# A fused attention and two-layer kernel: weight splits of layer 1 moved from GpSimd to ScalarE and VectorE, with a separate buffer for early conversions

## The chip, the cores and the metric

The kernel runs on one core of a Trainium2 chip. The metric is the device time of one execution in microseconds (us), median of three runs: 707.14 us, from 705.8 to 709.77. A core has TensorE (PE in the profile; its weight loads have a row of their own, PEld), VectorE (DVE), ScalarE (ACT), GpSimd (POOL) and SyncE (SP, which here issues nearly all DMAs). Each engine takes its instructions in a fixed order and waits on semaphores for the others.

## The reference, cut to what matters

Attention over 2 batches, 12 heads and 448 positions, with a 12 x 12 mixing of the heads before and after the softmax, gives x of 896 tokens by 768. Two feed-forward layers follow, each 768 to 2048 to 768, each with a pointwise function in the middle:

```python
h = x @ w_in                                 # layer 1
g = h * np.clip(h + 3.0, 0.0, 6.0) / 6.0
x = g @ w_out
h = x @ w_in2                                # layer 2
P = a[0] + a[1]*h + a[2]*h**2 + a[3]*h**3
Q = 1.0 + abs(b[0])*abs(h) + abs(b[1])*h**2
out = (P / (Q + 1e-6)) @ w_out2
```

The weights arrive as 64-bit floats, so each one is two 32-bit words in HBM.

## The kernel before, in words

**Split matmuls.** Every product of two fp32 matrices is done as three matmuls (`mm3`, lines 387 to 389): high part times high part, high times low, low times high. So each weight tile is needed as a rounded high part `wh` and a remainder `wl`.

**Units.** Weights come in units (`units`, line 392). Layer 1 has 16 units "in1" (one for each 128-wide slice f of the 2048) and 18 units "out1" (for each 128-wide output slice c of the 768, three pieces kk of 6, 6 and 4 slices f). Layer 2 has 16 "in2" and 16 "out2". A unit is 128 x 768 values (128 x 512 for kk = 2).

**What is done for a unit.** `load_unit` issues one DMA on SP (768 KB) into `wraw`, which has two buffers. `to_f32` turns 64-bit floats into fp32: one ScalarE pass (line 435) and three VectorE passes (437, 439, 443), into `wf`, which has two buffers. `split_pieces` then makes `wh` and `wl`, three buffers each: for layer 1 on GpSimd (459 the copy, 460 the subtraction), for layer 2 on ScalarE (462) and VectorE (463). Since `wh` and `wl` have three buffers, a unit can be split only after TensorE has finished the unit three places earlier.

**Order of the stages.** Attention runs from 0 to some 234 us in an order written by hand; the first four units of layer 1 are split inside it. Then come the "in1" slices f = 2 to 15 (lines 755 to 761; f = 0 and 1 are begun inside the hand-written order): for each f, 18 matmuls of 384 columns and 18 of 512 into two PSUM banks, which `act1` turns into `gh[f]` and `gl[f]` with ScalarE (561, 565) and VectorE (563, 566). Then come the six "out1" slices c (762 to 777), 96 matmuls each, whose results go to `XH` and `XL` (775 to 777). Layer 2 follows from some 467 us to the end. Outside the hand-written part the order of the instructions of each engine is set by a scheduler when the program is built; it is a fixed list on the chip.

**Early conversions.** `pre_slot` (735) uses the time of layer 1 to convert ten "in2" units of layer 2, f = 2 to 11, from 64-bit to fp32 and to write them back to HBM. Three calls make one conversion: load the raw unit into `wpre` (744), run `to_f32` into a `wf` buffer (748, 749), store it with a DMA (752). It is called once for each f and once for each (c, kk). The buffer is the same two-buffer `wf` that layer 1's own units go through.

**The temporaries of `act1`** come from `tmp` (550), four buffers of 128 x 512: two are used for each half of an f.

Of the kernel before, what the change touches and what calls it, by code (L numbers as in the profile page):

```python
# [7 lines left out]
F32 = mybir.dt.float32  # L8
# [40 lines left out]
def fused_kernel(  # L49
# [334 lines left out]
    pools = {}  # L384
# [7 lines left out]
    units = [("in1", f, 0) for f in range(KF)]  # L392
# [36 lines left out]
    def to_f32(t, n, w):  # L429


        tv = t[:, : 2 * n].rearrange("p (a two) -> p a two", two=2)
        hw, lw = tv[:, :, 1], tv[:, :, 0]
        wi = w.bitcast(I32)
        nc.scalar.activation(out=w, in_=hw.bitcast(F32), func=AF.Copy, scale=2.0**-112)  # L435
        yield
        nc.vector.tensor_scalar(out=wi, in0=wi, scalar1=3, scalar2=None, op0=ALU.logical_shift_left)  # L437
        yield
        nc.vector.scalar_tensor_tensor(  # L439
            out=wi, in0=hw, scalar=icst[:, 0:1], in1=wi, op0=ALU.bitwise_and, op1=ALU.bitwise_or  # L440
        )
        yield
        nc.vector.scalar_tensor_tensor(  # L443
            out=wi, in0=lw, scalar=icst[:, 1:2], in1=wi, op0=ALU.logical_shift_right, op1=ALU.bitwise_or
        )
        yield

    def split_pieces(u):
        t, n = raws.pop(u)
        n *= 128  # L450
        if u[0] == "in2" and u[1] in pre:
            w = t
        else:
            w = pools["late"].tile([128, KD * 128], F32, tag="wf", bufs=2, name="wf")[:, :n]
            yield from to_f32(t, n, w)
        hv = pools["late"].tile([128, KD * 128], F32R, tag="wh", bufs=3, name="wh")[:, :n]
        lv = pools["late"].tile([128, KD * 128], F32R, tag="wl", bufs=3, name="wl")[:, :n]
        if u[0] in ("in1", "out1"):
            nc.gpsimd.tensor_scalar(out=hv, in0=w, scalar1=1.0, scalar2=0.0, op0=ALU.mult, op1=ALU.add)  # L459
            nc.gpsimd.tensor_tensor(out=lv, in0=w, in1=hv.bitcast(F32), op=ALU.subtract)  # L460
        else:
            nc.scalar.activation(out=hv, in_=w, func=AF.Copy)
            nc.vector.tensor_tensor(out=lv, in0=w, in1=hv.bitcast(F32), op=ALU.subtract)  # L463
        if u[0] == "out2":
            for d, x in zip(wsp[u[1]], (hv, lv)):
                nc.sync.dma_start(out=d, in_=x.bitcast(F32))
        else:
            hv, lv = (x.rearrange("p (a b) -> p a b", b=128) for x in (hv, lv))
        spl[u] = (hv, lv)

    def split_unit(u):
        for _ in split_pieces(u):
            pass
# [74 lines left out]
            pass  # L548

    def tmp(name, n):  # L550
        return pools["gp"].tile([128, 512], F32, tag="tmp", bufs=4, name=name)[:, :n]

    def act1(f, p):
        t0, t1 = PARTS[p]
        n = t1 - t0
        hp = hps.pop((f, p))[:, :n]
        if f not in gh:
            gh[f] = pools["gp"].tile([128, NT], F32R, tag=f"gh{f}", name=f"gh{f}")
            gl[f] = pools["gp"].tile([128, NT], F32R, tag=f"gl{f}", name=f"gl{f}")
        t = tmp("t1", n)  # L560
        nc.scalar.activation(out=t, in_=hp, func=AF.Relu, bias=bias3)
        g = tmp("g1", n)
        nc.vector.scalar_tensor_tensor(out=g, in0=t, scalar=6.0, in1=hp, op0=ALU.min, op1=ALU.mult)  # L563
        o = gh[f][:, t0:t1]
        nc.scalar.activation(out=o, in_=g, func=AF.Copy)  # L565
        nc.vector.tensor_tensor(out=gl[f][:, t0:t1], in0=g, in1=o.bitcast(F32), op=ALU.subtract)  # L566
# [19 lines left out]
    for C, (b, r0, n, G) in enumerate(chunks):  # L586
# [21 lines left out]
        for s in range(G):  # L608
# [51 lines left out]
            if C == PRE and s == LATE - 1:  # L660
                flush()
                front.release()
                pools["late"] = tc.alloc_tile_pool(name="late", bufs=1, side="right", reuse_waits="tile")
                load_units(1)
                wpieces = (p for u in units[:4] for p in split_pieces(u))
# [46 lines left out]
    gp = pools["gp"] = tc.alloc_tile_pool(name="gp", bufs=1, reuse_waits="tile")  # L712
# [20 lines left out]
    slot, held = [0], {}  # L733

    def pre_slot():
        i, k = divmod(slot[0] - 1, 3)
        slot[0] += 1
        if not 0 <= i < len(PRE2):
            return
        f = PRE2[i]  # L740
        n = KD * 128
        if k == 0:
            held["t"] = gp.tile([128, 2 * n], I32, tag="wpre", name=f"wpre{f}")
            nc.sync.dma_start(
                out=held["t"].rearrange("p (a b) -> p a b", b=256), in_=w2i[:, :, f * 256 : f * 256 + 256]
            )
        elif k == 1:
            held["w"] = pools["late"].tile([128, n], F32, tag="wf", bufs=2, name="wf")
            for _ in to_f32(held["t"], n, held["w"]):
                pass  # L750
        else:
            nc.sync.dma_start(out=pre[f], in_=held["w"])

    ui = 2
    for f in range(2, KF):
        advance(ui)
        for p in range(2):
            run(gemm1(f, p, bank(f"h1_{f}_{p}")))
            act1(f, p)
        pre_slot()  # L760
        ui += 1
    for c in range(KD):
        hp = [bank(f"y1_{c}_{p}") for p in range(2)]
        for kk, (k0, k1) in enumerate(KSP):
            advance(ui)
            wh, wl = spl.pop(("out1", c, kk))
            for f in range(k0, k1):
                for p, (t0, t1) in enumerate(PARTS):
                    mm3(hp[p][:, : t1 - t0], wh[:, f - k0, :], wl[:, f - k0, :], gh[f][:, t0:t1], gl[f][:, t0:t1],
                        f == 0, f == KF - 1)  # L770
            pre_slot()
            ui += 1
        for p, (t0, t1) in enumerate(PARTS):
            y = tmp("y", t1 - t0)
            nc.scalar.activation(out=y, in_=hp[p][:, : t1 - t0], func=AF.Copy, scale=1.0 / 6.0)
            nc.vector.tensor_copy(out=XH[:, c, t0:t1], in_=y)
            nc.vector.tensor_tensor(out=XL[:, c, t0:t1], in0=y, in1=XH[:, c, t0:t1].bitcast(F32), op=ALU.subtract)
# [5 lines left out]
    gp = pools["gp2"] = tc.alloc_tile_pool(name="gp2", bufs=1, reuse_waits="tile")  # L783
# [57 lines left out]
    for f in range(KF):  # L841
        advance(ui, AHEAD2)
        w = spl.pop(("in2", f, 0))
# [155 lines left out]
```

## Time and profile before

| | |
|---|---|
| median of 3 runs | 707.14 us (705.8 to 709.77) |
| the profiled execution | 707.37 us |
| its span in the trace | 705.66 us |
| granted TensorE clock over the span | 0.998 of full speed |
| TensorE busy | 689.6 us, 98% |
| VectorE busy | 557.2 us, 79% |
| ScalarE busy | 411.1 us, 58% |
| GpSimd busy | 256.9 us, 36% (none after some 463 us) |

Three stretches matter. From 244.4 to 346.4 us TensorE does f = 2 to 15 of "in1" (called the h stretch here), from 346.4 to 467.5 us the "out1" slices (the y stretch), and from 467.5 us to the end layer 2. In the rows, tile names of the first stretch are `h`, `g`, `gh`, `gl`; of the second `y`. A time behind "<-" in square brackets is how long the engine was idle before an instruction, and for what it waited. A matmul's row lasts longer than the step to the next one, since matmuls overlap; the step is read from the start times.

### The profile page before, as it was taken

To read this page: it belongs to the slowest core of one execution; us is meant where nothing else is said; L and a number is where in the kernel's file an instruction comes from. 1 tells how busy PE (TensorE), PEld (TensorE's weight loads), DVE (VectorE), ACT (ScalarE), POOL (GpSimd) and SP (SyncE) were. 2 spreads that over 40 slices of the span, in tenths; PEclk is the share of its full clock that TensorE was granted. 3 is DMA by queue.
4 is the path that set the end of the run, shared out by engine and by line. 5 is a ranking of instruction groups with operands and counts; after the bars stand their busy time and mean duration, and the time that the engine had idled before them with its cause. 6 is when DMAs were issued, how large, how long until landed. Compare 5 with 4: busy or idle time off the path is not lost.

```text
span 705.7 us, 12410 instructions
## 1 busy us (share of the span) xinstructions
PE 689.6 (98%) x4461; PEld 617.5 (88%) x4461; DVE 557.2 (79%) x934; ACT 411.1 (58%) x851; POOL 256.9 (36%) x255
## 2 busy tenths in 40 slices
PE   8989999999999999999999999999999999999997
PEld 4768888888889888989888888889999999999997
DVE  6845585665657689889987777879999899989991
ACT  6757887887787343434342212227766667679851
POOL 2876775877776334323434543410000000000000
PEclk9999999999999999999999999999999999999999
DMA  5636486545394444555345544466575584755522
GB/s 206 226 111 176 142 209 190 166 142 166 119 260 123 148 144 136 155 157 156 121 151 177 186 160 141 140 247 236 209 270 186 196 267 144 242 196 202 188 82 89
DMA packets 76032, 122.81 MB, mean 174 GB/s; under 512 B 6804, under 2 KB 56260, under 8 KB 75972
## 3 DMA queue, kind: packets, MB, share of 16 engines
q1 hardware_dynamic: 75684, 121.66, 53.9%
q8 instruction: 35, 0.57, 0.3%
q10 hardware_dynamic: 288, 0.37, 0.1%
q14 instruction: 25, 0.20, 0.1%
HBM read 83.39 MB, written 19.27 MB: 145 GB/s over the span
## 4 chain that ended last, share of the span: by engine, by line
PE 60%; DVE 24%; DMA 7%; ACT 4%; issue 4%; POOL 0%; POOLq 0%; SPq 0%; ACTq 0%; DVEq 0%
PE A L341 9%; DVE wf L439 6%; PE h L389 6%; PE h L388 6%; PE h L387 6%; DVE wf L443 6%; PE acc L387 6%; PE acc L389 6%; PE acc L388 6%; PE X L363 5%; DMA pre<-wf 4%; PE sc L271 4%; DVE gl L566 4%; PE M L306 3%; DVE wf L437 3%
## 5 line engine op out<-in xcount | busy, mean ns | idle before, releaser
L389 PE MATMUL h<-xh,wl 128*128 128x512 f32 (+1 forms) x384 | 139.9, 364 | 0.8 <-DVE wl L463 0.8
L388 PE MATMUL h<-xl,wh 128*128 128x512 f32 (+1 forms) x384 | 139.5, 363 | 0.0
L387 PE MATMUL h<-xh,wh 128*128 128x512 f32 (+1 forms) x384 | 139.5, 363 | 0.0
L435 ACT ACTIVATE wf<-wraw 128x768 f32<-128x768 f32 (+1 forms) x56 | 48.7, 878 | 96.0 <-DMA pre<-wf 57.2
L296 POOL TENSOR_TENSOR sl<-full,sh 120x448 fp32r<-120x448 f32 x87 | 99.9, 1148 | 7.2
L310 DVE TENSOR_REDUCE st<-M 120x1 f32<-120x448 f32 x90 | 56.1, 623 | 51.3 <-PE M L308 51.1
L341 PEld LDWEIGHTS A<-wr,e 120*112 120x112 f32 x720 | 87.2, 178 | 7.9 <-ACT wr L325 3.9
L341 PE MATMUL A<-wr,e 120*112 120x120 f32 x720 | 89.7, 268 | 2.2 <-ACT wr L325 2.2
L459 POOL TENSOR_SCALAR wh<-wf 128x768 fp32r<-128x768 f32 (+1 forms) x34 | 32.6, 959 | 141.4 <-DVE wf L443 140.5
L312 ACT ACTIVATE e<-M,st 120x448 f32<-120x448 f32 x90 | 57.1, 635 | 42.7 <-DVE st L310 37.1
L389 PEld LDWEIGHTS h<-xh,wl 128*128 128x128 f32 x384 | 72.0, 188 | 9.0 <-DVE wl L463 1.1
L387 PEld LDWEIGHTS h<-xh,wh 128*128 128x128 f32 x384 | 72.1, 188 | 7.5
L388 PEld LDWEIGHTS h<-xl,wh 128*128 128x128 f32 x384 | 72.1, 188 | 7.6
L389 PE MATMUL y<-gh,wl 128*128 128x384 f32 x192 | 70.1, 365 | 2.6 <-POOL wl L460 2.6
L388 PE MATMUL y<-gl,wh 128*128 128x384 f32 x192 | 70.2, 366 | 1.0 <-DVE gl L566 1.0
L294 POOL TENSOR_SCALAR sh<-full 120x448 fp32r<-120x448 f32 x87 | 54.3, 624 | 46.1 <-PE M L307 21.5
L387 PE MATMUL y<-gh,wh 128*128 128x384 f32 x192 | 69.9, 364 | 0.0
L460 POOL TENSOR_TENSOR wl<-wf,wh 128x768 fp32r<-128x768 f32 (+1 forms) x34 | 67.5, 1985 | 2.8
L439 DVE SCALAR_TENSOR_TENSOR wf<-wraw,icst,wf 128x768 int32<-128x768 int32 (+1 forms) x56 | 61.7, 1103 | 0.7
L437 DVE TENSOR_SCALAR wf<-wf 128x768 int32<-128x768 int32 x66 | 43.1, 654 | 22.6 <-ACT wf L435 22.3
L443 DVE SCALAR_TENSOR_TENSOR wf<-wraw,icst,wf 128x768 int32<-128x768 int32 (+1 forms) x56 | 57.7, 1032 | 0.6
L565 ACT ACTIVATE gh<-g 128x384 fp32r<-128x384 f32 (+1 forms) x32 | 18.5, 579 | 60.3 <-DVE g L563 60.0
(114 smaller groups left out, 1521.7 us busy)
## 6 DMA issues: line engine op xcount, KB each, us to landing
wraw<-in_moe_w_out_dram SPq DMA_DIRECT2D x28, 768.0 KB
wraw<-in_moe_w_in_dram SPq DMA_DIRECT2D x22, 768.0 KB
full<-stg SPq DMA_DIRECT2D x60, 210.0 KB
vraw<-in_v_dram SPq DMA_DIRECT2D x42, 224.0 KB
wpre<-in_moe_w_in_dram SPq DMA_DIRECT2D x10, 768.0 KB
w2h<-wh SPq DMA_DIRECT2D x16, 384.0 KB
w2l<-wl SPq DMA_DIRECT2D x16, 384.0 KB
ws<-w2h SPq DMA_DIRECT2D x16, 384.0 KB
```

What stands on the lines that cost most here:

```text
L294: eng.tensor_scalar(out=sh[:r], in0=s[:r], scalar1=1.0, scalar2=0.0, op0=ALU.mult, op1=ALU.add)
L296: return lambda: eng.tensor_tensor(out=sl[:r], in0=s[:r], in1=sh[:r].bitcast(F32), op=ALU.subtract)
L310: nc.vector.tensor_reduce(out=st[:r, 0:1], in_=mt[:r, :S], op=ALU.max, axis=AX.X, negate=True)
L312: nc.scalar.activation(out=e[:r], in_=mt[:r, :S], func=AF.Exp, bias=st[:r, 0:1], accum_out=st[:r, 1:2])
L341: nc.tensor.matmul(av[:, jc], lhsT=e[:r, jc * JP : (jc + 1) * JP], rhs=wr[:r, :, :rr], start=True, stop=True)
L387: nc.tensor.matmul(o, lhsT=wh, rhs=mh, start=first, stop=False)
L388: nc.tensor.matmul(o, lhsT=wh, rhs=ml, start=False, stop=False)
L389: nc.tensor.matmul(o, lhsT=wl, rhs=mh, start=False, stop=last)
L437: nc.vector.tensor_scalar(out=wi, in0=wi, scalar1=3, scalar2=None, op0=ALU.logical_shift_left)
L439: nc.vector.scalar_tensor_tensor(out=wi, in0=hw, scalar=icst[:, 0:1], in1=wi, op0=ALU.bitwise_and, op1=ALU.bitwise_or)
L443: nc.vector.scalar_tensor_tensor(out=wi, in0=lw, scalar=icst[:, 1:2], in1=wi, op0=ALU.logical_shift_right, op1=ALU.bitwise_or)
L460: nc.gpsimd.tensor_tensor(out=lv, in0=w, in1=hv.bitcast(F32), op=ALU.subtract)
```

## The change

Three lines change. Only the first four units of layer 1 are still split on GpSimd; the other 12 "in1" units and all 18 "out1" units are split by ScalarE (line 462) and VectorE (463), as those of layer 2 already were. The early conversions write to a buffer `wfp` of their own, one of 128 x 768 in the pool `gp`, instead of a `wf` buffer. To make room in `gp`, `tmp` has three buffers instead of four.

```diff
@@ split_pieces
-        if u[0] in ("in1", "out1"):
+        if u in units[:4]:
             nc.gpsimd.tensor_scalar(out=hv, in0=w, scalar1=1.0, scalar2=0.0, op0=ALU.mult, op1=ALU.add)
             nc.gpsimd.tensor_tensor(out=lv, in0=w, in1=hv.bitcast(F32), op=ALU.subtract)
         else:
             nc.scalar.activation(out=hv, in_=w, func=AF.Copy)
             nc.vector.tensor_tensor(out=lv, in0=w, in1=hv.bitcast(F32), op=ALU.subtract)
@@ tmp
-        return pools["gp"].tile([128, 512], F32, tag="tmp", bufs=4, name=name)[:, :n]
+        return pools["gp"].tile([128, 512], F32, tag="tmp", bufs=3, name=name)[:, :n]
@@ pre_slot
-            held["w"] = pools["late"].tile([128, n], F32, tag="wf", bufs=2, name="wf")
+            held["w"] = gp.tile([128, n], F32, tag="wfp", name="wfp")
```

The order of TensorE's instructions stays as it was. On VectorE, ScalarE and SP it changes inside layer 1. First VectorE in the h stretch, around the second half of f = 9 (`g_4102` and `gl_4074` are its activation; `wpre_4639` is the raw data of an early conversion; a minus is a row of before, a plus one of now):

```order
 L566 TENSOR_TENSOR gl_4074<-g_4077,gh_4073 128x384
-L437 TENSOR_SCALAR wf<-wf 128x768
-L439 SCALAR_TENSOR_TENSOR wf<-wraw,icst,wf 128x768
-L443 SCALAR_TENSOR_TENSOR wf<-wraw,icst,wf 128x768
+L437 TENSOR_SCALAR wfp<-wfp 128x768
+L439 SCALAR_TENSOR_TENSOR wfp<-wpre_4639,icst,wfp 128x768
+L463 TENSOR_TENSOR wl<-wf,wh 128x768
 L563 SCALAR_TENSOR_TENSOR g_4102<-t_4100,h_9_1_4081 128x512
+L443 SCALAR_TENSOR_TENSOR wfp<-wpre_4639,icst,wfp 128x768
 L566 TENSOR_TENSOR gl_4074<-g_4102,gh_4073 128x512
```

An early conversion that stood in the y stretch before (`wpre_4639` is the sixth) now stands here, and a subtraction L463 for each unit is new. In the order of now all ten early conversions stand ahead of the last `gl` of f = 15; in the order of before five do.

Next VectorE in the y stretch, between the results of c = 3 and of c = 4 (`wpre_5227` is the tenth early conversion, 128x512 is a piece kk = 2):

```order
-L437 TENSOR_SCALAR wf<-wf 128x768
-L439 SCALAR_TENSOR_TENSOR wf<-wpre_5227,icst,wf 128x768
-L443 SCALAR_TENSOR_TENSOR wf<-wpre_5227,icst,wf 128x768
+L463 TENSOR_TENSOR wl<-wf,wh 128x768
 L437 TENSOR_SCALAR wf<-wf 128x512
 L439 SCALAR_TENSOR_TENSOR wf<-wraw,icst,wf 128x512
-L437 TENSOR_SCALAR wf<-wf 128x768
 L443 SCALAR_TENSOR_TENSOR wf<-wraw,icst,wf 128x512
+L463 TENSOR_TENSOR wl<-wf,wh 128x768
+L437 TENSOR_SCALAR wf<-wf 128x768
```

The conversion is gone from here and each unit's subtraction stands in the list between the conversions of later units.

Last ScalarE at the same place (L775 writes the results of c = 4 out of PSUM):

```order
-L435 ACTIVATE wf<-wpre_5227 128x768
+L462 ACTIVATE wh<-wf 128x768
 L435 ACTIVATE wf<-wraw 128x512
+L462 ACTIVATE wh<-wf 128x768
 L435 ACTIVATE wf<-wraw 128x768
 L775 ACTIVATE y<-y_4_0_5090 128x384
+L462 ACTIVATE wh<-wf 128x512
 L775 ACTIVATE y<-y_4_1_5091 128x512
```

The ScalarE pass of the early conversion, which stood in front of those of the layer's own units, is gone from here, and the copies to `wh` are new.

On SP the ten pairs of a store and a raw load of the early conversions move with them: they stand one or two loads of layer 1 apart instead of three, and the 12 loads of "out1" after the last store have none between them. Behind the last `gl` of f = 15 no order of layer 2 changes.

## Rows read from the trace of the kernel before

**Rows 1.** Busy time by stretch: TensorE, weight loads, VectorE, ScalarE, GpSimd; clock, DMA share, GB/s.
```profile
244.40:346.40 102.00, 102.00 (x506) 91.28 (x505) 91.45 (x98) 41.06 (x67) 39.58 (x27) 1.00 0.50 151
346.40:467.50 121.10, 117.55 (x578) 103.71 (x577) 99.55 (x105) 29.93 (x45) 51.44 (x34) 1.00 0.51 166
467.50:705.70 238.20, 233.47 (x1250) 220.62 (x1248) 210.97 (x328) 157.63 (x264) 0.00 (x0) 1.00 0.56 194
```
**Rows 2.** Timeline of TensorE: start, length, instruction; the first matmuls of f = 8 and 9.
```profile
302.60 0.33 PE L387 MATMUL h<-xh,wh 128*128 128x384 f32 x1
...
309.87 0.33 PE L387 MATMUL h<-xh,wh 128*128 128x384 f32 x1
```
**Rows 3.** Waits from 222 to 476 us: who for whom, us, times, longest.
```profile
PEld y L389 <- POOL wl L460: 4.2, 5, 1.1
...
PE y L389 <- POOL wl L460: 2.6, 5, 0.8
...
PEld y L388 <- DVE gl L566: 1.4, 1, 1.4
...
PEld h L389 <- DVE wl L463: 1.1, 1, 1.1
...
PE y L388 <- DVE gl L566: 1.0, 1, 1.0
PE h L389 <- DVE wl L463: 0.8, 1, 0.8
```
**Rows 4.** Timeline of TensorE at the start of c = 4 of "out1".
```profile
421.56 0.34 PE L387 MATMUL y<-gh,wh 128*128 128x384 f32 x1
421.73 0.34 PE L388 MATMUL y<-gl,wh 128*128 128x384 f32 x1
422.88 0.44 PE L389 MATMUL y<-gh,wl 128*128 128x384 f32 x1 [0.81 <-POOL wl L460]
```
**Rows 5.** Waits from 345 to 467 us.
```profile
ACT wf L435 <- DMA pre<-wf: 50.3, 6, 10.2
```
**Rows 6.** Chain of waits: start, us, what.
```profile
357.51 5.80 DMA wraw<-in_moe_w_out_dram
```
**Rows 7.** Timeline of VectorE, then of GpSimd at the same time.
```profile
258.99 0.69 DVE L566 TENSOR_TENSOR gl<-g,gh 128x512 fp32r<-128x512 f32 x1 [0.23 <-ACT gh L565]
...
295.59 0.55 DVE L437 TENSOR_SCALAR wf<-wf 128x768 int32<-128x768 int32 x1
...
297.45 0.55 DVE L566 TENSOR_TENSOR gl<-g,gh 128x384 fp32r<-128x384 f32 x1
...
300.26 2.32 DVE L566 TENSOR_TENSOR gl<-g,gh 128x512 fp32r<-128x512 f32 x1
...
300.01 2.02 POOL L460 TENSOR_TENSOR wl<-wf,wh 128x768 fp32r<-128x768 f32 x1
```
**Rows 8.** Groups of VectorE in the h stretch: busy us, mean ns, idle before.
```profile
L566 DVE TENSOR_TENSOR gl<-g,gh 128x512 fp32r<-128x512 f32 x13 | 22.5, 1734 | 4.9 <-ACT gh L565 4.9
L439 DVE SCALAR_TENSOR_TENSOR wf<-wraw,icst,wf 128x768 int32<-128x768 int32 x13 | 19.0, 1460 | 0.2
L437 DVE TENSOR_SCALAR wf<-wf 128x768 int32<-128x768 int32 x17 | 13.0, 762 | 0.0
L443 DVE SCALAR_TENSOR_TENSOR wf<-wraw,icst,wf 128x768 int32<-128x768 int32 x12 | 12.2, 1013 | 0.1
...
L566 DVE TENSOR_TENSOR gl<-g,gh 128x384 fp32r<-128x384 f32 x11 | 7.7, 699 | 0.0
L563 DVE SCALAR_TENSOR_TENSOR g<-t,h 128x384 f32<-128x384 f32 x12 | 6.6, 546 | 5.8 <-ACT t L561 5.8
L439 DVE SCALAR_TENSOR_TENSOR wf<-wpre,icst,wf 128x768 int32<-128x768 int32 x4 | 4.4, 1108 | 0.0
```
**Rows 9.** Groups of VectorE in the y stretch.
```profile
L443 DVE SCALAR_TENSOR_TENSOR wf<-wpre,icst,wf 128x768 int32<-128x768 int32 x6 | 13.5, 2242 | 0.2
...
L439 DVE SCALAR_TENSOR_TENSOR wf<-wpre,icst,wf 128x768 int32<-128x768 int32 x6 | 8.3, 1382 | 0.2
```
**Rows 10.** The splits of layer 2: duration ns, shortest, median, longest.
```profile
L463 DVE TENSOR_TENSOR wl<-wf,wh x22: 948/952/959, 467.9 to 624.7; 128x768 fp32r<-128x768 f32 x22
L462 ACT ACTIVATE wh<-wf x22: 837/848/859, 465.2 to 623.8; 128x768 fp32r<-128x768 f32 x22
```

## The prediction

> **What bounds the kernel now.** I read the busy times by stretch first, then the start times of TensorE's matmuls, then its waits, and only then the engines that it waits for. TensorE is busy for all 102.0 us of the h stretch and for 117.6 of the 121.1 us of the y stretch, at the full granted clock of 1.00 (its 2.4 GHz level) [rows 1]. "Busy" could hide gaps, so the start times are the check: one f begins at 302.60 us and the next at 309.87 [rows 2]. That is 7.27 us, and 14 times that is 101.8 us, so the h stretch of 102.0 us is 14 steps of this length and almost nothing else. TensorE therefore sets the time there, although VectorE is busy for 91.5 of the 102.0 us and GpSimd's work lengthens it.
>
> In the y stretch TensorE does wait. Five waits for GpSimd's `wl` (2.6 us together), one for VectorE's last `gl` (1.0) and one for the `wl` of the first unit of layer 2 (0.8) make 4.4 us [rows 3]. A matmul's row covers part of a gap: at 421.73 us the next matmul begins 1.15 us later where the step is 0.17 (421.56 to 421.73), so 0.98 us is lost and the wait row says 0.81 [rows 4]. With 0.17 us more for each of the seven waits the loss is 4.4 + 1.2 = 5.6 us. The weight loads put their own waits at 4.2 + 1.4 + 1.1 = 6.7 us [rows 3], the other end. What stands behind these waits is not GpSimd's speed alone: ScalarE stood still for 50.3 us in the y stretch, since its conversion pass L435 wanted a `wf` buffer that an early conversion's store still read [rows 5], and whatever came behind in its fixed order stood with it.
>
> **The separate buffer.** Now that store holds only `wfp`, so the 50.3 us of waiting go. In the y stretch no early conversion is left, so VectorE sheds two groups of 13.5 and 8.3 us there [rows 9]. The first subtraction of each c no longer waits for anything that ends shortly before it is needed. With three buffers, a unit is split as soon as TensorE has finished the unit three places earlier, which leaves two units of lead: in the h stretch 2 x 7.27 = 14.5 us; in the y stretch 121.1 less 5.6 us over 96 slices is 1.2 us a slice, and two units are at least 10 slices, 12 us. In the new order the L463 stand at those places, so five waits fall from 3.4 us (2.6 + 5 x 0.17) to nothing. The wait for `gl` of f = 15 (1.2 us) came from VectorE and ScalarE being late at the end of the h stretch behind a weight load of 5.80 us that ScalarE stood at [rows 6]. The first unit of layer 2 (1.0 us) was split late for the same chain of late `wf` buffers. Both should go.
>
> **The splits on VectorE and ScalarE.** This is the step that could cost. GpSimd's subtraction stretches VectorE's instructions when they overlap: the 512-wide `gl` takes 0.69 us alone and 2.32 while GpSimd's L460 runs [rows 7]. In the h stretch this is, from the group means [rows 8] less what the same form takes free [rows 7], for L439 the 1013 ns of L443: 13 x (1734 - 690) = 13.6 us, 13 x (1460 - 1013) = 5.8, 17 x (762 - 550) = 3.6, 11 x (699 - 550) = 1.6, 4 x (1108 - 1013) = 0.4, together 25.0 us. Free of it VectorE needs 91.5 - 25.0 = 66.5 us. Added are 14 subtractions of 0.95 us [rows 10], 13.3 us, and six early conversions that came later before (four had run in this stretch [rows 8]), 6 x (0.55 + 1.01 + 1.01) = 15.4 us. The sum is 95.2 us of 102.0: VectorE stays about as full as before, with the same kind of slack. Its idle time behind ScalarE was 4.9 + 5.8 = 10.7 us [rows 8]; if all of that stays, it needs 105.9 us and ends the stretch 3.9 us late, well inside the lead of 14.5 us. The unit prices that I take are those at the bottom of their rows; their top ends are the third rival below.
>
> ScalarE goes from 41.1 us [rows 1] by 14 x 0.85 [rows 10] and six passes of about 0.9 (estimate: the same 768 values as L462) to some 58 of 102.0 us. Its fixed order is the real risk: a copy to `wh` waits until TensorE has released the buffer, and the activation of the next half stands behind it. In the order that wait ends with the same half of f that the activation wants, so it costs about the copy itself, 0.85 us, with 14.5 us in hand.
>
> In the y stretch VectorE loses at least 21.8 us and gains some 12 x 0.95 + 6 x 0.7 (estimate for 512 columns, 0.95 x 512/768 and a little) = 15.6, out of 99.6 of 121.1 us: no bound.
>
> **The transfers.** Six more early conversions in the h stretch are 6 x (768 + 384) KB = 7.1 MB in 102 us, 69 GB/s on top of 151; layer 2 runs at 194 as a mean [rows 1]. On SP a store waits for its conversion, and the loads behind it wait too. A load issued late by such a wait of 3 or 4 us and then taking 5.80 us is still inside the 14.5 us that two buffers allow. I cost it at nothing; without that cover it would be some 2 to 3 us for each of a few units.
>
> **tmp with three buffers.** A half's first temporary now waits for the `gl` of two halves before; that is done half an f or more earlier. Nothing.
>
> **Sum.** 707.37 us of the profiled execution less 5.6 is 701.8. I keep 0.2 us for small waits that take their place and forecast 702.0 us. Against the median of 707.14, which the profiled execution meets within 0.03%, that is 0.7% less. Its own range from the two ends of the waits (4.4 and 6.7 us) and some 0.7 us of spread is 700.0 to 703.7.
>
> **TensorE's headroom, read in another way.** The rows show the step of 7.27 us with GpSimd and VectorE busy beside it, and weight loads at 91.3 of 102.0 us [rows 1, 2]. The Trainium skill (Perfetto Trace Analysis, Identifying the Most-Contended Engine) holds matmul busy time to be a poor measure of TensorE's headroom and takes the busy share of the weight loads instead. By that rule TensorE has 10.7 us free in the h stretch and 17.4 in the y stretch, and a change that relieves its suppliers could win up to 28 us. By the rows, layer 2, where GpSimd does nothing, has 1250 matmuls in 238.2 us, 0.19 us each beside 0.20 (102.0 / 506) in the h stretch, where more of them have 512 columns; relieved of GpSimd the step is no shorter.
>
> **Rivals.**
> 1. *The wait moves instead of going.* `wl` now comes from an engine with a fixed order, so L463 can be stuck behind conversions whose data are late. The five waits then stay in part, or a few appear in the h stretch. For it: VectorE at 95 of 102 us, and the early conversions as a cycle of store, load and conversion that ScalarE stands at. Against it: leads of 12 us and more. Half the gain lost gives 704.6, all of it 707.
> 2. *Faster by more than the waits.* TensorE speeds up once its suppliers are ahead; up to 28 us as worked out above, 679 us. Against it stands the unvarying step.
> 3. *Slower: VectorE becomes the bound of the h stretch.* If the long forms are not GpSimd's doing (DMA writes or TensorE's reads instead), the 25.0 us stay and VectorE needs 91.5 + 13.3 + 15.4 + 10.7 = 130.9 us of 102.0. It is 28.9 us late; 14.5 are covered, 14.4 are lost, and with the y stretch's gain kept the time is 707.4 + 14.4 - 3.4 = 718 us. It decides from about half of the 25.0 us on (118.4 us needed, 16.4 late, 1.9 lost). Against it: the long `gl` begins with GpSimd's L460 and ends with it [rows 7].
>
> **How the numbers follow.** The forecast has 0.70, rival 1 0.17, rival 2 0.03, rival 3 0.10. What a measurement here can tell from no change is about 0.5%, so "faster" means below 703.6 us: 0.64 of the forecast's 0.70, 0.02 of rival 1 and rival 2's 0.03 give 0.69. "Slower" is above 710.7, rival 3 with little else: 0.09. The rest, 0.22, is the same. For eight in ten I reach from 700.0 to 705.6, which takes in the forecast's own range and the better half of rival 1, and leaves out rivals 2 and 3.
>
> **What would show it.** In the profile after, the waits of TensorE's matmuls for `wl` and `gl` in the y stretch should be gone, an f should still take 7.27 us, and the y stretch should last some 116.5 us instead of 121.1. The 512-wide `gl` should take 0.69 us throughout after the fourth unit, VectorE be busy for some 95 of the 102 us of the h stretch and at most 93 us of the y stretch (99.6 - 21.8 + 15.6), and ScalarE's wait for the store be gone. I am wrong if TensorE waits in the h stretch, if its step changes, or if the y stretch keeps gaps at the start of each c.

## The result, and the profile after

The first measurement gave 698.39 us (median of 4 runs, 697.88 to 701.0) against 706.77 us for the kernel before: a ratio of 0.988, 95% interval 0.984 to 0.992. That is 3.6 us below the forecast and 1.6 us below the low end of its range. A second measurement (e4 below, the same kernel, 6 runs beside 23 of before) gave 700.68 us, ratio 0.991 (0.990 to 0.993), a gain of 6.1 us, inside the range. Both intervals lie below 1. One execution each of e5 (848 us), e8 (1135 us) and e10 (3203 us) was in a slow state and is left out of the times and ratios below. The profiled execution after took 697.88 us with a span of 696.1 us.

The busy times by stretch answer to [rows 1], with the same columns: TensorE, weight loads, VectorE, ScalarE, GpSimd, clock, DMA share, GB/s. The h stretch, the y stretch and layer 2:

```profile
241.63:343.63 102.00, 102.00 (x506) 91.52 (x506) 97.34 (x136) 58.23 (x90) 3.25 (x2) 1.00 0.68 211
343.63:459.49 115.86, 115.86 (x578) 104.01 (x576) 70.31 (x99) 36.46 (x52) 0.00 (x0) 1.00 0.41 138
459.49:696.10 236.61, 233.16 (x1249) 220.65 (x1247) 208.73 (x325) 156.57 (x263) 0.00 (x0) 1.00 0.54 187
```

The h stretch is as long as before, with VectorE even fuller (97.3 of 102 us). The y stretch lasts 115.86 us instead of 121.1, all of it TensorE's own work, and layer 2 is 1.6 us shorter. The waits from 220 to 476 us, which answer to [rows 3] and [rows 5]; these are the two largest of ScalarE, the largest of VectorE, and ScalarE's wait for the loads of the early conversions:

```profile
ACT wh L462 <- PE y L388: 46.6, 10, 6.4
ACT wf L435 <- DVE wl L463: 34.0, 25, 3.3
DVE wl L463 <- ACT wh L462: 30.5, 9, 6.3
...
ACT wfp L435 <- DMA wpre<-in_moe_w_in_dram: 12.5, 8, 3.0
```

No row with TensorE waiting is left, and the wait for a store is gone. ScalarE now stands at its copies until TensorE gives a `wh` buffer back (46.6 us): the suppliers wait for TensorE, and not the other way. The same three matmuls as in [rows 4], now:

```profile
416.05 0.34 PE L387 MATMUL y<-gh,wh 128*128 128x384 f32 x1
416.22 0.34 PE L388 MATMUL y<-gl,wh 128*128 128x384 f32 x1
416.40 0.34 PE L389 MATMUL y<-gh,wl 128*128 128x384 f32 x1
416.57 0.39 PE L387 MATMUL y<-gh,wh 128*128 128x512 f32 x1
```

The fourth row is the next matmul. The step before L389 is 0.18 us, where it was 1.15. ([Rows 4] were labelled wrongly ahead of the prediction: they are not the start of c = 4 but of the last piece, kk = 2, of c = 3. The five waits for `wl` stand at the piece kk = 2 of c = 1 to 5, the one unit of 128x512.) VectorE's groups in the h stretch answer to [rows 8]:

```profile
L463 DVE TENSOR_TENSOR wl<-wf,wh 128x768 fp32r<-128x768 f32 x14 | 15.0, 1068 | 0.0
...
L566 DVE TENSOR_TENSOR gl<-g,gh 128x512 fp32r<-128x512 f32 x14 | 9.6, 688 | 0.0
...
L439 DVE SCALAR_TENSOR_TENSOR wfp<-wpre,icst,wfp 128x768 int32<-128x768 int32 x9 | 9.4, 1045 | 0.2
...
L437 DVE TENSOR_SCALAR wf<-wf 128x768 int32<-128x768 int32 x13 | 7.2, 554 | 1.2 <-ACT wf L435 1.2
L566 DVE TENSOR_TENSOR gl<-g,gh 128x384 fp32r<-128x384 f32 x13 | 7.2, 551 | 0.3 <-ACT gh L565 0.3
```

All the stretched forms are short again: `gl` of 512 columns takes 0.69 us where its mean was 1.73.

**Where the profiled difference of 9.6 us (705.7 to 696.1) comes from.** Read from start times: 2.6 us ahead of the first matmul of `h` (at 222.80 us before, 220.23 after), 0.3 from there to the first `y`, 5.2 in the y stretch, 1.1 at the first unit of layer 2, and 0.4 behind it. The first of these is not the change's. At 36 to 40 us, in the attention part, TensorE waits for GpSimd's L294, and in some executions the granted clock falls behind that. Columns as above, before and then after:

```profile
36.00:40.00 4.00, 1.17 (x7) 0.59 (x6) 1.16 (x4) 1.01 (x3) 1.74 (x3) 1.00 0.76 232
40.00:46.00 6.00, 5.98 (x33) 4.82 (x34) 2.64 (x9) 3.88 (x10) 5.67 (x8) 0.72 0.01 3
```

```profile
36.00:40.00 4.00, 2.47 (x18) 1.86 (x18) 1.93 (x5) 1.09 (x4) 2.66 (x4) 1.00 0.74 232
40.00:46.00 6.00, 5.93 (x43) 4.61 (x43) 3.32 (x12) 4.45 (x13) 5.75 (x8) 1.00 0.06 16
```

In the execution before TensorE was busy for 1.17 of 4 us there, and the clock of the next 6 us was 0.72; after, 2.47 of 4 and 1.00. Inside those 6 us the clock before was near its lower level of 1.2 GHz for a time:

```profile
41.00:44.60 3.60, 3.60 (x18) 2.85 (x17) 1.53 (x8) 2.87 (x8) 3.43 (x5) 0.53 0.02 5
```

The second profiled execution of the changed kernel (e4) has 0.72 again from 40 to 46 us, and starts `h` at 223.09 us. So this is chance from one execution to the next, and the profiled pair overstates the gain by some 2.6 us.

### The profile page after: what moved, and what is told of

It is laid out like the page before. It is cut to its first block, busy times and chain, and to the rows that moved or that the text cites. A ratio compares the mean times of both kernels' runs of the same rounds, so it can differ in the third digit from the quotient of the medians.

```text
span 696.1 us, 12343 instructions
## 1 busy us (share of the span) xinstructions
PE 686.3 (99%) x4460; PEld 616.2 (89%) x4461; DVE 532.7 (77%) x964; ACT 433.8 (62%) x881; POOL 168.2 (24%) x195
## 4 chain that ended last, share of the span: by engine, by line
PE 93%; DMA 2%; DVE 2%; issue 1%; ACT 1%; POOL 0%; SPq 0%; POOLq 0%; DVEq 0%
PE h L389 11%; PE h L388 11%; PE h L387 11%; PE A L341 9%; PE acc L387 6%; PE acc L389 6%; PE acc L388 6%; PE y L388 6%; PE y L387 6%; PE y L389 6%; PE X L363 5%; PE sc L271 4%; PE M L306 3%; PE M L308 2%; PE M L307 2%; DMA vraw<-in_v_dram 1%
## 5 line engine op out<-in xcount | busy, mean ns | idle before, releaser
L389 PE MATMUL h<-xh,wl 128*128 128x512 f32 (+1 forms) x384 | 139.7, 364 | 0.0
L462 ACT ACTIVATE wh<-wf 128x768 fp32r<-128x768 f32 (+1 forms) x52 | 42.6, 819 | 62.0 <-PE y L388 46.6
L389 PEld LDWEIGHTS h<-xh,wl 128*128 128x128 f32 x384 | 72.1, 188 | 7.6
L435 ACT ACTIVATE wf<-wraw 128x768 f32<-128x768 f32 (+1 forms) x56 | 49.5, 883 | 42.9 <-DVE wl L463 40.8
L463 DVE TENSOR_TENSOR wl<-wf,wh 128x768 fp32r<-128x768 f32 (+1 forms) x52 | 49.6, 954 | 32.4 <-ACT wh L462 32.4
L389 PE MATMUL y<-gh,wl 128*128 128x384 f32 x192 | 69.5, 362 | 0.0
L294 POOL TENSOR_SCALAR sh<-full 120x448 fp32r<-120x448 f32 x87 | 54.0, 620 | 43.5 <-PE M L307 20.6
L443 DVE SCALAR_TENSOR_TENSOR wf<-wraw,icst,wf 128x768 int32<-128x768 int32 (+1 forms) x56 | 56.5, 1011 | 0.7
L439 DVE SCALAR_TENSOR_TENSOR wf<-wraw,icst,wf 128x768 int32<-128x768 int32 (+1 forms) x56 | 55.9, 999 | 0.9
L348 ACT ACTIVATE at<-A 112x480 f32<-112x480 f32 x87 | 50.3, 579 | 1.8 <-PE A L341 1.8
L389 PE MATMUL acc<-ws,xl 128*128 128x384 f32 x128 | 42.8, 334 | 0.0
```

The lines of the kernel that those rows point to most:

```text
L294: eng.tensor_scalar(out=sh[:r], in0=s[:r], scalar1=1.0, scalar2=0.0, op0=ALU.mult, op1=ALU.add)
L348: aposts.append(lambda: nc.scalar.activation(out=o, in_=av, func=AF.Copy))
L389: nc.tensor.matmul(o, lhsT=wl, rhs=mh, start=False, stop=last)
L439: nc.vector.scalar_tensor_tensor(out=wi, in0=hw, scalar=icst[:, 0:1], in1=wi, op0=ALU.bitwise_and, op1=ALU.bitwise_or)
L443: nc.vector.scalar_tensor_tensor(out=wi, in0=lw, scalar=icst[:, 1:2], in1=wi, op0=ALU.logical_shift_right, op1=ALU.bitwise_or)
```

## The experiments

All on whole kernels, five rounds each unless said; ratios to the kernel before, which ran beside them (706.78 us with e1 to e4, 706.67 with e5 to e8, 706.37 with e9 to e11).

| run | us | ratio, 95% interval |
|---|---|---|
| e1 split edit alone | 699.84 | 0.991, 0.9895 to 0.9925 |
| e2 separate buffer (and `tmp` of three) alone | 707.5 | 1.0015, 0.9995 to 1.0036 |
| e3 `tmp` of three alone | 707.04 | 1.0008, 0.999 to 1.0025 |
| e4 the whole change again | 700.68 | 0.9914, 0.9897 to 0.9932 |
| e5 split edit, GpSimd subtracts for nothing | 717.4 | 1.0152, 1.0131 to 1.0173 |
| e6 whole, GpSimd copies `wh` | 699.48 | 0.9897, 0.9878 to 0.9917 |
| e7 whole, V loaded later | 699.49 | 0.9895, 0.9877 to 0.9913 |
| e8 whole, filler matmuls | 699.12 | 0.9898, 0.9878 to 0.9919 |
| e9 as e5, one round | 716.62 | 1.0141, 1.0106 to 1.0177 |
| e10 whole, GpSimd subtracts `wl` | 708.38 | 1.0029, 1.0013 to 1.0044 |
| e11 whole, each subtraction three times | 707.34 | 1.0011, 0.9992 to 1.0031 |

### Which edit does it: e1 to e4

Theory A is the prediction's: the waits come from the `wf` buffer that an early conversion's store still reads. Theory B: they come from GpSimd. e1 has only this line of the change, e3 only `tmp`, e2 `tmp` and the buffer:

```diff
e1  -        if u[0] in ("in1", "out1"):
    +        if u in units[:4]:
e3  -  tag="tmp", bufs=4
    +  tag="tmp", bufs=3
e2  as e3, and
    -            held["w"] = pools["late"].tile([128, n], F32, tag="wf", bufs=2, name="wf")
    +            held["w"] = gp.tile([128, n], F32, tag="wfp", name="wfp")
```

> Only the splits move to ScalarE and VectorE; the early conversions keep sharing the wf buffers and stay half in the y stretch. Theory A (the waits of TensorE in the y stretch come from the wf buffer that a store still reads): ScalarE still stands some 50 us for the store, most of the waits for wl stay, and the time is 704 to 707 us. Theory B (they come from GpSimd, which is slow and stretches VectorE): the waits are gone although ScalarE still stands for the store, and the time is that of the whole change, 698 to 699 us.

> Only the separate buffer and the three temporaries; all splits of layer 1 stay on GpSimd. Theory A: the waits of the y stretch fall by most of their 4.6 us of gaps; in the h stretch VectorE needs some 91.5 + 15.4 + 10.7 = 117.6 us of 102.0 with GpSimd's stretching still there, 1 us over the lead of 14.5 us, so 701 to 704 us. Theory B: the waits for GpSimd's wl stay and the time is 706 to 708 us.

> Only three temporaries instead of four. The lists of all engines stay as in the kernel before, so both theories expect no change, 706 to 707.5 us; it also shows how far two programs with the same lists differ, and how often TensorE's clock falls in the attention part (by half for 3.4 us in the profile of before, not in that of after), which I hold for chance: some of its executions should have it and some not.

> The whole change once more, timed closely. By the gaps of TensorE that went (6.5 us with the longer matmul behind each) the ratio should be 0.989 to 0.992 of before; a ratio of 0.988 or less would say that about 2 us more come from elsewhere, such as the attention part, where the profile of after is 2.6 us shorter.

The split edit alone gives the whole gain, and the separate buffer alone gives nothing. In e1 no wait of TensorE is left from 220 to 476 us, and its y stretch lasts 115.85 us. Although the early conversions still go through `wf`, the 50.3 us of [rows 5] are down to this (waits from 345 to 467 us of e1, then ScalarE at the conversion of the piece kk = 2 of c = 1):

```profile
ACT wf L435 <- DMA pre<-wf: 1.1, 4, 0.3
```

```profile
359.35 1.70 ACT L435 ACTIVATE wf<-wraw 128x512 f32<-128x512 f32 x2 [0.24 <-DMA pre<-wf]
```

This conversion begins 15.6 us after the first matmul of the y stretch (343.80 us); in the kernel before it began 29.3 us after it (375.76 and 346.48). Ahead of it ScalarE now has a copy at which it waits for TensorE (44.0 us for all copies from 345 to 467 us), and by then the store has landed. So the long wait for the store went together with the lateness of the whole chain, and no other buffer was needed to take it away; Theory A, that the buffer is what matters, falls. (Theory B had the time nearly right, but not that the store wait would go.) With e2 the five waits at kk = 2 do go, which Theory B had not foreseen either, but others take their place. TensorE's waits of e2 from 300 to 476 us, and the stretch in which they lie:

```profile
PE y L388 <- DVE gl L566: 1.8, 2, 1.6
PE y L387 <- DVE g L563: 1.0, 1, 1.0
PE y L387 <- ACT gh L565: 0.6, 1, 0.6
PE y L389 <- POOL wl L460: 0.4, 1, 0.4
```

```profile
344.00:372.00 28.00, 24.12 (x108) 20.11 (x107) 27.43 (x34) 11.74 (x19) 9.29 (x9) 0.95 0.41 135
```

TensorE is busy for 24.12 of these 28 us and VectorE for 27.43: VectorE is late with the last `g` and `gl`, which TensorE wants at the start of the y stretch. The buffer lets the early conversions run in the h stretch, and there GpSimd's subtraction stretches them. VectorE's groups of e2 in the h stretch (beside those of after, above):

```profile
L566 DVE TENSOR_TENSOR gl<-g,gh 128x512 fp32r<-128x512 f32 x12 | 13.8, 1146 | 0.0
L439 DVE SCALAR_TENSOR_TENSOR wf<-wraw,icst,wf 128x768 int32<-128x768 int32 x12 | 13.7, 1143 | 0.2
L439 DVE SCALAR_TENSOR_TENSOR wfp<-wpre,icst,wfp 128x768 int32<-128x768 int32 x8 | 13.2, 1653 | 0.2
```

`wfp` takes 1.65 us where it takes 1.05 in the changed kernel. The longest of the new waits ends with such a stretched instruction; TensorE, VectorE and GpSimd in e2:

```profile
368.61 0.50 PE L388 MATMUL y<-gl,wh 128*128 128x512 f32 x1 [1.60 <-DVE gl L566]
```

```profile
366.49 2.06 DVE L566 TENSOR_TENSOR gl<-g,gh 128x512 fp32r<-128x512 f32 x1 [0.16 <-ACT gh L565]
...
365.98 2.03 POOL L460 TENSOR_TENSOR wl<-wf,wh 128x768 fp32r<-128x768 f32 x1
```

At its 0.69 us this `gl` would have been there 1.4 us earlier. How the five waits of before came about can be followed in its trace; here for c = 1, kk = 2, one row each of ScalarE, VectorE and GpSimd, and of TensorE the late matmul and its next:

```profile
375.76 1.46 ACT L435 ACTIVATE wf<-wraw 128x512 f32<-128x512 f32 x2 [9.39 <-DMA pre<-wf]
...
378.05 0.74 DVE L443 SCALAR_TENSOR_TENSOR wf<-wraw,icst,wf 128x512 int32<-128x512 int32 x1
...
378.96 1.25 POOL L459 TENSOR_SCALAR wh<-wf 128x512 fp32r<-128x512 f32 x1 [6.86 <-DVE wf L443]
380.29 1.87 POOL L460 TENSOR_TENSOR wl<-wf,wh 128x512 fp32r<-128x512 f32 x1
...
382.21 0.44 PE L389 MATMUL y<-gh,wl 128*128 128x384 f32 x1 [0.15 <-POOL wl L460]
382.50 0.40 PE L387 MATMUL y<-gh,wh 128*128 128x512 f32 x1
```

The store, the conversion and then 1.25 + 1.87 us on GpSimd stand in one chain that ends at TensorE. Either edit removes these five waits; only the split edit brings no new ones. Whether the split edit does it by the shorter splits or by the end of the stretching, these runs do not divide.

### What it is about GpSimd: e5, e6, e9, e10

Theory C: GpSimd's subtraction, by stretching what VectorE does beside it, makes the splits late. Theory D: GpSimd was only one link too many between the conversion and `wl`. Theory C is tested by giving GpSimd the subtraction back with no one waiting for its result (e5, and e9, which is the same kernel; both on e1), Theory D by giving it back one link at a time (e6 the copy, e10 the subtraction). The edits, shortened; their added lines shift the line numbers of these kernels by one to three:

```diff
e5  (on e1, behind VectorE's subtraction)
    +  if u[0] in ("in1", "out1") and "gp" in pools:
    +      d = pools["gp"].tile([128, KD * 128], BF16, tag="dum", name="dum")[:, :n]
    +      nc.gpsimd.tensor_tensor(out=d, in0=w, in1=hv.bitcast(F32), op=ALU.subtract)
e6  (on the whole change, "in1" and "out1")
    -  nc.scalar.activation(out=hv, in_=w, func=AF.Copy)
    +  nc.gpsimd.tensor_scalar(out=hv, in0=w, scalar1=1.0, scalar2=0.0, op0=ALU.mult, op1=ALU.add)
e10 (on the whole change, "in1" and "out1")
    -  nc.vector.tensor_tensor(out=lv, in0=w, in1=hv.bitcast(F32), op=ALU.subtract)
    +  nc.gpsimd.tensor_tensor(out=lv, in0=w, in1=hv.bitcast(F32), op=ALU.subtract)
```

> The kernel with the split edit alone, and one thing more: for each weight unit of layer 1 from the fifth on, GpSimd also makes the subtraction w - wh and writes it to a tile that nothing reads. The orders of VectorE and ScalarE are those of the split edit alone. Theory C (GpSimd's subtraction stretches whatever VectorE does beside it, and this, not GpSimd's being a link of the chain to wl, is what made the splits late): VectorE's busy time in the h stretch goes from 91.8 us by some 15 to 25 up to the stretch's full 102 us or over, the 512-wide gl beside the idle subtraction takes 1.9 to 2.3 us and not 0.69, g falls behind TensorE by more than 10 us, waits of TensorE in the y stretch return and the ratio to the kernel before is 0.995 to 1.005. Theory D (the chain through GpSimd itself was late, VectorE had room): VectorE keeps its 102 us, no wait returns, the ratio stays at 0.991 within 0.002.

> The whole change, but wh of layer 1 from the fifth unit on is copied by GpSimd again; the subtraction stays on VectorE, whose order is the same. GpSimd is again a link of the chain to wl, with about 1.25 to 1.9 us a unit. Theory C (the subtraction on GpSimd was the harm): if the copy does not stretch VectorE, its 512-wide gl stays at 0.69 us, VectorE's busy time in the h stretch stays near 97 us, no wait of TensorE for wl returns and the ratio is 0.991 to 0.993. Theory D (the link through GpSimd was the harm): waits at the third column piece of a group return, at least half of the 5 to 6 us, ratio 0.995 or over. If the copy stretches VectorE as the subtraction does, gl rises to about 2 us as well and the waits return with it; then the two theories are not told apart by this run.

> The same kernel as e5_gpsimd_idle_work, for a profile at full clock (its first one had a granted clock of 0.75 from start to end). Theory C: VectorE's busy time in the h stretch is near 102 us instead of 91.8, the 512-wide gl beside the idle subtraction takes about 2 us, TensorE waits for wl or gl by 10 to 18 us in all in the h and y stretches, which is what the ratio of 1.015 wants; h or y is longer by as much. Rival: VectorE's forms are as short as in the split edit alone, and the loss comes from wf or wh buffers that GpSimd holds longer, so that ScalarE's L435 or L462 waits for GpSimd.

> The whole change, but wl of layer 1 from the fifth unit on is subtracted by GpSimd again; the copy stays on ScalarE, whose order is the same. This is the other half of the split edit. Theory C (the subtraction on GpSimd was the harm): as with the separate buffer alone, ratio 0.998 to 1.004, VectorE busy for 92 us or more of the h stretch with 13 instructions fewer than in the whole change, and waits for wl or gl are back. Theory D (any one link less in the chain is enough): 0.991 to 0.994.

The trace read here is that of e9. The useless subtraction costs 16 to 17 us against e1 (from 0.991 to 1.014 in e9 and 1.015 in e5, of 706.4 and 706.7 us), more than the 0.995 to 1.005 that I expected. It is also longer than the one that it stands for: 2.64 us in the mean, where L460 takes 1.98 in the h stretch before. In e9, VectorE's own subtraction in the h stretch, TensorE's waits from 300 to 476 us, and one pair of GpSimd and VectorE instructions:

```profile
L463 DVE TENSOR_TENSOR wl<-wf,wh 128x768 fp32r<-128x768 f32 x12 | 24.6, 2051 | 0.0
```

```profile
PE y L389 <- DVE wl L463: 9.8, 11, 2.0
PE h L389 <- DVE wl L463: 2.1, 2, 1.8
```

```profile
336.29 2.59 POOL L466 TENSOR_TENSOR dum<-wf,wh 128x768 bf16<-128x768 f32 x1 [5.60 <-ACT wh L462]
...
337.12 2.57 DVE L463 TENSOR_TENSOR wl<-wf,wh 128x768 fp32r<-128x768 f32 x1
```

L463 begins 0.83 us after GpSimd's subtraction and takes 2.57 us instead of 0.95; its mean is 2.05. All 13 waits of TensorE are for it. Part of the loss is another thing that the expectation named as the rival: ScalarE's L435 waited 23.9 us (9 times) for GpSimd to give a `wf` buffer back. The two act at once and the run does not divide them; it does show that a subtraction whose result nobody needs is enough to bring waits for `wl` back. VectorE's busy time, which I expected to rise to the full stretch, was 94.3 of 104.6 us: it got later, so it did fewer instructions in the same time (113 where e1 has 130).

The copy on GpSimd does no harm (0.9897), although GpSimd is a link of the chain again; the subtraction takes the whole gain (1.0029), although ScalarE still copies. Theory D, by which one link less would do, falls with e10. The copy and the subtraction differ in length, from 243 to 343 us of e6, VectorE first and then GpSimd (L463 is the copy there):

```profile
L569 DVE TENSOR_TENSOR gl<-g,gh 128x512 fp32r<-128x512 f32 x14 | 10.2, 730 | 0.0
...
L463 POOL TENSOR_SCALAR wh<-wf 128x768 fp32r<-128x768 f32 x14 | 14.8, 1059 | 77.8 <-PE h L388 42.3 <-DVE wf L443 19.9 <-DVE g L566 6.3
```

and in the same time of e10 (L464 is the subtraction):

```profile
L439 DVE SCALAR_TENSOR_TENSOR wfp<-wpre,icst,wfp 128x768 int32<-128x768 int32 x9 | 15.3, 1697 | 0.3
...
L464 POOL TENSOR_TENSOR wl<-wf,wh 128x768 fp32r<-128x768 f32 x11 | 24.3, 2208 | 62.7 <-DVE gl L567 31.3 <-ACT wh L462 27.0 <-DVE wfp L443 4.4
```

A copy takes 1.06 us and the subtraction 2.21, and what VectorE begins meanwhile lasts until after its end, so the shorter one holds less. In e10 the waits moved into the h stretch (3.2 + 2.8 us for `wh` and `wl`), which lasts 110.6 us there, while the y stretch has the undisturbed 115.9.

That the stretching of VectorE is what does the harm, e10 does not show. The stretch of e10 ahead of its first wait (317.7 us), and the largest wait of its ScalarE from 215 to 485 us for a buffer:

```profile
300.00:316.00 16.00, 16.00 (x80) 14.09 (x78) 12.52 (x16) 7.62 (x12) 3.19 (x2) 1.00 0.60 178
```

```profile
ACT wf L435 <- POOL wl L464: 45.2, 24, 2.2
```

VectorE had room, 12.52 of 16 us busy, and ScalarE stood 45.2 us until GpSimd's subtraction gave a `wf` buffer back. So there is a second way, the same as in e9: a subtraction of 2.2 us instead of 0.95 holds `wf` longer and makes the next conversions late. How much each way did is open. (The sum of such waits does not decide it: in e6 ScalarE waits 83.2 us for VectorE to give `wf` back, and nothing is lost.) Shown is that the subtraction must leave GpSimd; how it did harm there is in part argued. No run moves only the copy or only the subtraction in the kernel without `wfp`.

### How much room VectorE has: e11

The prediction held that being late by up to 14.5 us costs nothing. This run makes VectorE late with nothing else changed:

```diff
-            nc.vector.tensor_tensor(out=lv, in0=w, in1=hv.bitcast(F32), op=ALU.subtract)
+            for _ in range(3 if u[0] in ("in1", "out1") else 1):
+                nc.vector.tensor_tensor(out=lv, in0=w, in1=hv.bitcast(F32), op=ALU.subtract)
```

> The whole change with each subtraction of layer 1 on VectorE made three times (the same result). In the h stretch this is 14 x 2 x 0.95 = 26.6 us more on VectorE; six of the ten early conversions come later in this order, 6 x 2.57 = 15.4 us less, so VectorE needs some 97.3 + 11.2 = 108.5 us of 102. It would end the stretch 6.5 us later. If the lead of two units covers it, as the prediction had it (14.5 us): no wait of TensorE, 0.9914 within 0.002. If VectorE's slack is only what its idle time shows (about 5 us): 1 to 6 us lost around the start of the y stretch, 0.993 to 1.000.

The whole gain is gone. A piece of the h stretch of e11, before its first wait, and then TensorE's waits from 300 to 476 us (L464 is the subtraction):

```profile
300.00:316.00 16.00, 16.00 (x80) 14.24 (x79) 16.00 (x24) 7.84 (x13) 0.00 (x0) 1.00 0.41 124
```

```profile
PE h L389 <- DVE wl L464: 3.7, 2, 2.5
```

VectorE is busy for 16.00 of 16 us, and from the first `h` to the first matmul of layer 2 it takes 245.4 us (223.97 to 469.39) instead of 239.3 (220.23 to 459.49): 6.2 us lost, against an excess of 6.5 us that the expectation estimates. The waits came inside the h stretch (at 321.3 and 347.2 us), not at the start of y as I expected. By start times the two gaps are 2.65 + 1.41 = 4.1 us; the rest is slower matmuls behind them, mostly since a low clock followed the first (0.68 from 320 to 324 us). So the lead did not cover the excess: more than half of it became waits.

### The chance part: e7 and e8

Both try to take away the wait and the low clock behind 36 us: e7 issues the loads of V later, e8 gives TensorE six matmuls of no use where it stands still.

```diff
e7  -            if C == 0 and s == VAT:
    +            if C == 1 and s == 1:
e8  +            if C == 1 and s == 0:
    +                for i in range(FILL):          # FILL = 6, operands of zeros
    +                    nc.tensor.matmul(pf, lhsT=warm[:, :128], rhs=warm, start=(i == 0), stop=(i == FILL - 1))
```

> The whole change, with the loads of V (vraw) issued at a later place of the second chunk, behind the transfers of full<-stg instead of ahead of them. If the 2.6 us by which executions of one kernel differ ahead of the first h matmul come from full<-stg landing late beside these loads (TensorE stands 1.5 to 3.2 us at 36 to 40 us and its granted clock is then half for 3.4 us): TensorE's idle time there falls below 1 us, the granted clock of 36 to 46 us is 1.00, h starts at 220 to 220.5 us in the profile, and the time is 1 to 2.5 us under the whole change's, ratio 0.988 to 0.990. If it is chance of another kind: no change, 0.9914 within 0.002, and the idle time is 1.5 us or more.

> The whole change, with six bf16 matmuls of 512 columns on a tile of zeros put ahead of the mixing of the second chunk, where TensorE stands still at 36 to 40 us; their result is not used. If the halved clock behind that wait comes from TensorE standing still: the granted clock of 36 to 46 us is 1.00 in the profile though the wait for full<-stg stays, and the time is 0.5 to 1.7 us under the whole change's, ratio 0.989 to 0.991. If the clock falls for another reason, or the fill delays the mixing: 0 to 1 us slower, 0.9914 to 0.993.

Neither did what it was for. In e7 the wait at 36 to 40 us stayed and so did the low clock:

```profile
PE M L306 <- POOL sh L294: 1.7, 1, 1.7
```

```profile
36.00:40.00 4.00, 1.81 (x12) 1.24 (x10) 1.44 (x4) 1.43 (x4) 1.66 (x2) 0.96 0.04 15
40.00:46.00 6.00, 5.90 (x34) 5.16 (x35) 2.59 (x10) 3.41 (x10) 5.67 (x9) 0.74 0.47 150
```

The DMA queues were nearly empty meanwhile (0.04), so V's loads were not what L294 waited for in this execution. In e8 the fill ran and ended, TensorE still stood for 1.6 us behind it, and the clock of 40 to 46 us was 0.72. The medians, 699.49 and 699.12, are not measurably lower than e6's 699.48 on the same chip, which has neither edit. What makes L294 later in some executions stays open. No version was found that beats the changed kernel measurably: e1, e6, e7 and e8 are all as fast.

## Why the prediction was right or wrong

**What bounds the kernel.** Right. The step of an f is 7.27 us before [rows 2] and 7.26 after (300.04 to 307.30 us), TensorE sets the time, and it gains only what it waited for. Rival 2 is out: the h stretch is 102.00 us in both, so the weight loads' idle share [rows 1] was no headroom.

**The size.** The waits were worth 6.6 us in the trace (0.3 + 5.2 + 1.1), and 6.1 us by the medians of e4; the sum had 5.6. The term that was too small is the loss at a wait. The sum counted the gap ahead of the late matmul (5.6 us over seven waits; by start times 5.7 over eight, of which one, 0.16 us at 339 us, has no wait row). But the late matmul is itself slower: at 382.21 us above, the next begins 0.29 us later where the step is 0.17, so each wait costs 0.12 more, 0.9 us for eight. (The weight loads' 6.7 us, the other end of the prediction's range, came nearer to the 6.6.) Two smaller terms add to this: the forecast started from 707.37 us, where the kernel before measured 706.77, and kept 0.2 us for new waits, of which none came. By the medians the three are 0.5 + 0.6 + 0.2 = 1.3 us, and that is how far e4's 700.68 lies below the forecast.

The other 2.3 us of the first measurement are not the change's. Of the ten executions of the changed kernel in both measurements, the four with a mean granted clock of 1.000 took 697.9 to 698.6 us and the six at 0.994 to 0.998 took 699.8 to 702.0; the first measurement has three of the four, e4 one. Its own range allowed 0.7 us for spread, and its low end, 700.0, was too high for a median of four.

**The separate buffer.** This is the step that failed as a cause. It put the whole 5.6 us down to the buffer (and none to the splits). e2 has that buffer and gains nothing; e1 lacks it and gains all. The 50.3 us of [rows 5] were a large number on an engine that was not the bound, and I read them as the root. The five waits sat at the end of a chain of store, conversion and GpSimd, and I looked only at its longest idle link. (The L463 on VectorE, of the other edit, stood in that step's text, but no time was put down to it.)

**The splits on VectorE and ScalarE.** The prices were right, and the conclusion drawn from them was the wrong way round. VectorE needed 97.3 us in the h stretch against 95.2 forecast (L463 took 1.07 us there, not 0.95: 14 x 0.12 = 1.7); `gl` fell to 0.69 us and ScalarE rose to 58.2 us (58 forecast). The 25.0 us by which GpSimd stretched VectorE were worked out in this step, but only to show that the added work fits. The gain came from this step: e1 has it alone and gains all, and without the subtraction on GpSimd the new work is free. With it, e2 has VectorE full at the start of the y stretch (27.43 of 28 us) and waits behind a stretched `gl`; e10 loses the gain too, but with VectorE not full, so the stretching is shown at one wait of e2, and not as the only cause. The Trainium skill has the mechanism (SBUF — State Buffer, Who interferes with whom): a VectorE instruction with two inputs in SBUF contends with a GpSimd instruction that reads SBUF. The trace agrees for `gl` (0.69 and 2.32 us in [rows 7]) and for L463 (0.95 and 2.57 in e9).

**The lead of 14.5 us.** Wrong. e11, with VectorE some 6.5 us short by estimate, waited 4.1 us and lost 6.2. Rival 3 was to decide only from 16.4 us late on; by e11 the gain is gone long before, and VectorE now has 4.7 us left in the h stretch (97.3 of 102.0). The chance given to "slower" was low for a change with so little room.

**The transfers and `tmp`.** Right: 211 GB/s in the h stretch (220 forecast) with no wait of TensorE behind it, and e3, with the order of before, takes as long as before.

**What would show it.** No wait of TensorE from the h stretch to the first unit of layer 2, y at 115.9 us (116.5), VectorE at 70.3 us there (at most 93) and the store wait gone all came out. These marks fitted the wrong cause as well as the right one; only the edits apart could tell them apart.

## What to carry to other kernels

A long wait on an engine that does not set the time is a symptom until an experiment makes it a cause: follow the chain to the matmul that was late and ask for every link whether shortening it alone would do. Where two engines work side by side, compare the same form alone and beside the other; a form that takes three times as long there makes moving the other engine's work cheaper than its price list says. A lead in buffers, counted as free room on an engine that is nearly full on average, wants a run that uses it up, as e11 does here.

## What the runs showed of the hardware

- VectorE's subtraction beside GpSimd's (e9) takes 2.05 us in the mean and 2.6 at most, 0.95 alone; a 768-column copy on GpSimd (e6), at 1.06 us, raised the mean of the 512-wide `gl` only from 0.69 to 0.73 us.
- The step of a matmul behind a wait is 0.11 to 0.12 us longer than usual at the eight places of the kernel before (382.21 us above), so a short wait costs TensorE more than its row says.
- In the attention part the clock of 40 to 46 us was low (0.72 to 0.74) in seven profiled executions, in which TensorE's wait for L294 was 1.5, 1.6, 1.6, 1.7, 2.3, 2.6 and 3.4 us, and 1.00 in five, in which it was 0.7 to 1.2 us (e5 left out). It is seen at this one place, behind work of the same kind, and is no rule for others: in e10 TensorE was busy for only 1.09 of the 4 us from 316 to 320, and the clock of the next 8 us was 1.00, while behind its second stand there (1.50 of 4 us busy from 342 to 346) the clock of the next 4 us was 0.63.
